# Attention with a feed-forward on one core: split reciprocals, a new order of products, an earlier first pair and earlier stores

## The chip, the core and the metric

The kernel runs on one core of a Trainium2 chip. TensorE multiplies matrices and writes its results to eight banks of PSUM; VectorE (DVE), ScalarE (ACT) and GpSimd (POOL) do the elementwise work, and GpSimd does not read PSUM here. SyncE (SP) and ACT issue DMAs. The metric is the device time of one execution in microseconds (us), less is better. All data are float32.

## The reference

```python
def rmsnorm(x, g):
    return x / np.sqrt(np.mean(x * x, axis=-1, keepdims=True) + 1e-06) * g
# q, k, v: (batch 8, heads 12, seq 448, dim 64)
scores = 1.0 / np.sqrt(64) * rmsnorm(q, g_q) @ rmsnorm(k, g_k).transpose(0, 1, 3, 2)
attn = np.exp(scores - scores.max(-1, keepdims=True))
attn = attn / (attn.sum(-1, keepdims=True) + 1e-09)
x = (attn @ v).transpose(0, 2, 1, 3).reshape(8 * 448, 768)
h = np.maximum(x @ w_in, 0.0)          # w_in (768, 2048)
out = h * h @ w_out                    # w_out (2048, 768)
```

## The kernel before, in words

**Two programs and a branch.** The kernel reads the gains `g_q` and `g_k`, multiplies them, and sets a flag when their largest product is small enough for exponentials without the subtraction of a maximum. Every engine loads the flag and branches (L67, L68). With this data the branch without `shift` runs.

**Attention.** 48 pairs of heads, i = 0 to 47, are worked on one after the other, each in two visits (n = 0 and 1) of two key chunks each. For a pair, SP loads q and k (`load_qk`, two pairs ahead), ACT squares them (`square`), VectorE sums the squares and GpSimd takes the power -1/2 and scales q (`normalize`); k's scale goes into the exponential instead. TensorE transposes q and k (`turn`, L178), VectorE and ACT copy the results out (`qT`, `kT`). `weigh` makes four scores matmuls per visit (L198) and ACT their exponentials (L200). One visit set later `attend` multiplies by the values (L244). Row sums of the weights come from matmuls with ones: for the first two batches chunk by chunk (L251), for the others (`alone` is false) from sums of the four chunks that `add_up` makes (L212), head 0 on GpSimd, head 1 on VectorE. `denominators` puts them into bank 3 (L259) and ACT copies that to `xT` (L263); `invert` takes the reciprocal on VectorE (L274) and `finish` multiplies the values by it, reading their bank (L283).

**Feed-forward.** Two batches are one group u, 0 to 3. Both matrix products use a scheme of seven products (Strassen's, in Winograd's form): `make_x_forms` makes the sums of the activations that it needs (L311, VectorE and GpSimd in turn), and the weights are converted from their loaded form once, during the first half of the run (`convert`: three ACT operations, four on VectorE, then sums and a store), and reloaded from DRAM in later groups. A group has four blocks. A block has two rounds of seven *first products* (`first_products`, three matmuls each, L382) whose results ACT copies (`part`, L389) or VectorE adds up to `hid` (`hidden`, L403, then Relu and Square on ACT, L404 and L405), and then *second products* (`second_products`: four parts for the rest rows, L428, sums of `hid`, L440, and three rounds of seven, two matmuls each, L452), which VectorE adds to `acc` (L485, L469; in block 0 ACT copies).

**Banks.** The products share banks 5 to 7 in three roles, listed first in `PRODUCTS`; a product with `first` false adds to what its bank holds. A bank may be written again once ACT or VectorE has read it. `turn_roles` says which bank has which role in the next round.

**The order.** It is written out by hand: each engine does its instructions in the program's order. Group u's products are a generator (`stream`), and the attention of the next two batches is spread among them: `run` draws products until a cost is reached, 18 for a first product and 10 for a second, and after each draws a conversion if one is due, x forms if a group of four `xT` is complete, and one task off the list `tasks`. `visit_among` does the matmuls and exponentials of a visit at once and puts VectorE's part on that list. A group costs 2008 and has 24 visits, so six lie in a block: two in its first products, one between first and second products, two in the second, one at its end. Pairs 0 to 11 run before any product (`visit_alone`), and group 3 runs alone at the end.

**Stores.** At the end of a group `store` writes the seven tiles `acc` (L496), all on SP.

Of the kernel before, what the change touches and what calls it, by code (L numbers as in the profile page):

```python
# [2 lines left out]

# [30 lines left out]
def kernel(  # L34
# [18 lines left out]
    D = q.shape[3]  # L53
    const = ctx.enter_context(tc.tile_pool(name="const", bufs=1))
    g_rows = const.tile([1, 2, D], F32, name="g_rows")
    g_most = const.tile([1, 1], F32, name="g_most")
    bounded = const.tile([1, 1], I32, name="bounded")
    for n, g in enumerate((g_q, g_k)):
        nc.scalar.dma_start(g_rows[:, n], g.rearrange("(one d) -> one d", one=1))
    nc.vector.tensor_tensor(out=g_rows[:, 0], in0=g_rows[:, 0], in1=g_rows[:, 1], op=ALU.mult)  # L60
    nc.vector.tensor_reduce(
        out=g_most, in_=g_rows[:, 0], axis=AX.X, op=ALU.max, apply_absolute_value=True
    )
    nc.vector.tensor_scalar(
        out=bounded, in0=g_most, scalar1=MOST_G, scalar2=None, op0=ALU.is_le
    )
    flag = nc.values_load(bounded, min_val=0, max_val=1)  # L67
    with tc.If(flag > 0) as either:  # L68
        program(tc, q, k, v, g_rows[:, 0], moe_w_in, moe_w_out, out, shift=False)
    with either.Else():  # L70
        program(tc, q, k, v, g_rows[:, 0], moe_w_in, moe_w_out, out, shift=True)
# [3 lines left out]
def program(ctx, tc, q, k, v, g_row, moe_w_in, moe_w_out, out, shift):  # L75
    nc = tc.nc

    B, H, S, D = q.shape
# [15 lines left out]
    small = ctx.enter_context(tc.tile_pool(name="small", bufs=8))  # L94
# [4 lines left out]
    ident = const.tile([P, P], F32, name="ident")  # L99
    ones = const.tile([CP, D], F32, name="ones")  # L100
    g = const.tile([P, 1], F32, name="g")
    minus_half = const.tile([CP, 1], F32, name="minus_half")
# [12 lines left out]
    loaded, values, squared, normal, turned = {}, {}, {}, {}, {}  # L115
# [7 lines left out]
    def load_qk(i):  # L123
        b, c = pairs[i]
        qk = io.tile([CP, 2, 2 * NJ, D], F32, name="qk", tag="qk")
        for x, rows in enumerate((q, k)):
            for e in range(2):
                nc.sync.dma_start(
                    qk[:, x].rearrange("p (j h) d -> p j h d", h=2)[:, :, e],
                    rows[b, 2 * c + e].rearrange("(p j) d -> p j d", j=NJ),  # L130
                )
        loaded[i] = qk
# [10 lines left out]
    def square(i):  # L143
        squares = [
            att.tile([CP, 2 * NJ, D], F32, name="squares", tag="squares") for _ in range(2)
        ]
        for x in range(2):
            nc.scalar.activation(squares[x], loaded[i][:, x], AF.Square)
        squared[i] = squares

    def normalize(i):

# [647 lines left out]
```

## Time and profile before

| what | before |
|---|---|
| median of 3 runs | 1597.87 us (1596.63 to 1598.27) |
| the profiled execution | 1598.84 us, span of its instructions 1597.0 us |
| granted TensorE clock, mean | 0.980 |
| reciprocals, L274 | 36 of 2946 ns, and 12 of 2953 ns (attention alone) |
| exponentials, L200 | 384 of 634 ns |
| bytes moved by DMA | 164.65 MB, 31.4% of 16 engines' span |

The page has one row for each engine's busy time. A row of waits reads: who waited, for what, us in total, how often, the longest. A row of a timeline reads: start, duration, engine, line, operation, tile written and tiles read, shapes, how many rows are merged, and in brackets how long the engine was idle before and what ended that. A matmul of the program is two rows in the trace, and its end is modelled, so a merged row ends a little after the next may start.

### The profile page before, as it was taken

Reading aid. Unit: us, or ns where it says so; the run is one execution under the profiler, and the core shown is the slowest. Engines: PE = TensorE matmul, PEld = TensorE weight load, DVE = VectorE, ACT = ScalarE, POOL = GpSimd, SP = SyncE. Lnnn points to the kernel's source line nnn. Section 1 sums busy time; section 2 is a strip of 40 time slices with the busy share of each in tenths; the row PEclk is TensorE's granted clock in tenths of the full one; section 3 lists DMA queues with packets and bytes.
Section 4 is the critical chain, followed back from the end, with each engine's and each line's share of the span. In section 5 each row is a group of like instructions: output and inputs, shape, how many; then the busy total and the mean of one; then the engine's idle time right before and its main releaser. Section 6 shows DMA issues by size and latency. Waiting matters only on the chain.

```text
span 1597.0 us, 14972 instructions
## 1 busy us (share of the span) xinstructions
PE 1508.5 (94%) x5204; PEld 733.1 (46%) x5204; DVE 845.9 (53%) x1234; ACT 632.9 (40%) x1197; POOL 450.1 (28%) x298
## 2 busy tenths in 40 slices
PE   5999999889889899999999989999999989999997
PEld 2333444344444344544445444544445444555554
DVE  3897685775876753535454554436446263223323
ACT  4775465725716224342342413433251412231130
POOL 3454542342332422323222332322232130000000
PEclk9999999999999999999999999999999999999999
DMA  4554143542533325132323206132230305132122
GB/s 101 168 150 160 43 120 94 176 135 67 186 122 126 106 76 168 44 131 64 101 89 106 95 12 206 55 105 93 96 104 6 120 34 183 41 142 84 65 79 72
DMA packets 131801, 164.65 MB, mean 103 GB/s; under 512 B 92804, under 2 KB 115844, under 8 KB 123524
## 3 DMA queue, kind: packets, MB, share of 16 engines
q1 hardware_dynamic: 131712, 163.60, 31.4%
q8 instruction: 43, 0.70, 0.2%
q14 instruction: 42, 0.34, 0.1%
q10 hardware_dynamic: 4, 0.00, 0.0%
HBM read 128.98 MB, written 34.60 MB: 102 GB/s over the span
## 4 chain that ended last, share of the span: by engine, by line
PE 81%; DVE 13%; ACT 2%; issue 2%; POOL 0%; SPq 0%; DMA 0%; ACTq 0%; DVEq 0%; POOLq 0%
PE bank L382 29%; PE bank L452 24%; PE bank L198 10%; PE bank L244 9%; PE bank L428 4%; DVE xT L274 3%; PE bank L251 2%; PE bank L178 2%; DVE acc L485 2%; PE bank L259 2%; DVE sum L212 1%; DVE xT L311 1%; DVE sums L440 1%; DVE hid L403 1%; DVE in_sb L567 1%
## 5 line engine op out<-in xcount | busy, mean ns | idle before, releaser
L382 PE MATMUL bank<-xT,in_sb 128*128 128x448 f32 x1344 | 526.7, 546 | 7.1 <-ACT part L389 7.1
L382 PEld LDWEIGHTS bank<-xT,in_sb 128*128 128x128 f32 x1344 | 251.6, 192 | 258.1 <-issue 244.8
L200 ACT ACTIVATE wT<-bank,rr 112x448 f32<-112x448 f32 x384 | 211.9, 634 | 339.5 <-PE bank L198 338.3
L485 DVE TENSOR_TENSOR acc<-acc,bank 128x384 f32<-128x384 f32 x324 | 173.2, 548 | 203.5 <-PE bank L452 170.1
L452 PE MATMUL bank<-out_sb,hid 128*128 128x384 f32 x768 | 268.2, 495 | 5.5 <-DVE acc L485 5.5
L452 PE MATMUL bank<-out_sb,sums 128*128 128x384 f32 x576 | 211.1, 510 | 30.7 <-DVE acc L485 29.4
L403 DVE TENSOR_TENSOR hid<-bank,part 128x448 f32<-128x448 f32 x96 | 59.9, 624 | 307.2 <-PE bank L382 178.6
L161 POOL TENSOR_TENSOR rr<-ms,minus_half 112x16 f32<-112x16 f32 x48 | 140.1, 2918 | 267.4 <-DVE ms L157 246.4
L452 PEld LDWEIGHTS bank<-out_sb,hid 128*128 128x128 f32 x768 | 144.8, 192 | 116.3 <-issue 18.9
L198 PE MATMUL bank<-qT,kT 64*112 64x448 f32 x768 | 179.5, 571 | 10.7 <-ACT xT L263 9.0
L244 PE MATMUL bank<-wT,vt 112*64 112x448 f32 x768 | 169.7, 552 | 3.3 <-DVE xT L283 3.3
L452 PEld LDWEIGHTS bank<-out_sb,sums 128*128 128x128 f32 x576 | 109.4, 197 | 115.5 <-DVE acc L485 40.8
L404 ACT ACTIVATE hid<-hid 128x448 f32<-128x448 f32 x128 | 73.8, 576 | 202.1 <-DVE hid L403 202.1
L212 POOL TENSOR_TENSOR sum<-wT 112x448 f32<-112x448 f32 x36 | 40.9, 1136 | 379.8 <-ACT wT L200 379.8
L389 ACT COPY part<-bank 128x448 f32<-128x448 f32 x128 | 67.9, 530 | 151.8 <-PE bank L382 151.8
L198 PEld LDWEIGHTS bank<-qT,kT 64*112 64x112 f32 x768 | 63.6, 175 | 114.8 <-issue 64.5
L212 POOL TENSOR_TENSOR sum<-sum,wT 112x448 f32<-112x448 f32 x72 | 83.0, 1153 | 110.1 <-ACT wT L200 107.2
L274 DVE RECIPROCAL xT<-xT 128x448 f32<-128x448 f32 x36 | 106.1, 2946 | 11.4 <-ACT xT L263 11.4
L440 POOL TENSOR_TENSOR sums<-hid,sums 128x768 f32<-128x768 f32 x16 | 29.9, 1866 | 240.8 <-DVE sums L440 240.8
L244 PEld LDWEIGHTS bank<-wT,vt 112*64 112x64 f32 x768 | 50.2, 137 | 97.1 <-issue 81.1
L428 PE MATMUL bank<-out_sb,hid 128*128 128x384 f32 x256 | 91.6, 514 | 0.0
L212 DVE TENSOR_TENSOR sum<-wT 112x448 f32<-112x448 f32 x36 | 37.5, 1041 | 96.3 <-ACT wT L200 96.3
(56 smaller groups left out, 1222.6 us busy)
## 6 DMA issues: line engine op xcount, KB each, us to landing
out_sb<-out_forms SPq DMA_DIRECT2D x24, 1536.0 KB, 7.3
in_sb<-in_forms SPq DMA_DIRECT2D x24, 1344.0 KB, 6.1
words<-in_moe_w_in_dram SPq DMA_DIRECT2D x32, 384.0 KB, 3.8
words<-in_moe_w_out_dram SPq DMA_DIRECT2D x32, 384.0 KB, 3.2
out_forms<-out_sb SPq DMA_DIRECT2D x8, 1536.0 KB, 6.9
qk<-in_q_dram SPq DMA_DIRECT2D x96, 112.0 KB, 3.0
qk<-in_k_dram SPq DMA_DIRECT2D x96, 112.0 KB, 3.1
vt<-in_v_dram SPq DMA_DIRECT2D x48, 224.0 KB, 3.9
```

The lines of the kernel that those rows point to most:

```text
L161: nc.gpsimd.tensor_tensor(out=rr.rearrange("p x r -> p (x r)"), in0=ms, in1=minus_half.to_broadcast([CP, 4 * NJ]), op=ALU.pow,)
L198: nc.tensor.matmul(sc, lhsT=kT[r, ts(m, CP)], rhs=qT[r, :], start=True, stop=True)
L200: nc.scalar.activation(weights[i, e, m], sc, AF.Exp, scale=normal[i][1][:, 2 * m + e : 2 * m + e + 1])
L212: engine.tensor_tensor(out=sums[i, e], in0=left, in1=weights[i, e, m], op=ALU.add)
L244: nc.tensor.matmul(av[ds(e * D, D), :], lhsT=values[i][:, e, m, :], rhs=weights[i, e, m], start=m == 0, stop=m == NJ - 1,)
L274: nc.vector.reciprocal(out=dens[i], in_=den)
L382: nc.tensor.matmul(ps, lhsT=w_sb[:, IN.index(left), c, :], rhs=forms[u, c][right], start=first and c == 0, stop=c == NK - 1, skip_group_ch ...
L403: nc.vector.tensor_tensor(out=dst, in0=left, in1=right, op=op)
L404: nc.scalar.activation(dst, dst, AF.Relu)
L428: nc.tensor.matmul(ps, lhsT=flat[a][:, t, ds(FULL, P)], rhs=w_sb[t][:, 2 * a + half, :], start=(a, t) == parts[0], stop=(a, t) == parts[-1],)
L452: nc.tensor.matmul(ps, lhsT=lefts[left][:, t, ts(tt, P)], rhs=w_sb[t][:, OUT.index(right), :], start=first and t == 0, stop=t == 1, skip_g ...
L485: nc.vector.tensor_tensor(out=acc, in0=acc, in1=ps, op=ALU.add)
```

## The change

1. **Ahead of the branch.** Identity, ones, the loads of pair 0 (q on SP, k on ACT's queue), a first Exp that loads ACT's table, and pair 0's norm are moved ahead of the flag. q and k of pair 0 get separate squares (in PSUM), means and powers of 8 numbers a row, and VectorE scales q. A class `Rows` holds loading and norm for both parts.
2. **Tasks.** A reciprocal is two, of 224 columns each, as two tasks; the norm is three tasks (mean of q, mean of k, power and scaling); all three additions of a head's weights are made after the second visit instead of one after the first and two after the second. After a first product two tasks are taken, after a second product one.
3. **Order of products.** In the first products P4 comes before P7; ACT copies P4 and both last sums follow P7. In the second P4 comes before P3. The roles turn so that two products lie between uses of a bank.
4. **Stores.** In a group's last block a tile is stored two or more products after its last addition. The very last tile goes out on SP and ACT.
5. **Pools.** `sum` has 2 buffers instead of 4, `ms` and `rr` 5 each, `squares` one for q and one for k.

```diff
+    rows = Rows(nc, SimpleNamespace(io=const, small=const), q, k, ones, minus_half)
+        rows.load(0, (nc.sync, nc.scalar))
+        nc.scalar.activation(g_most, ones[0:1, 0:1], AF.Exp)
+        make_identity(nc, ident)
...
+        for x in range(2):
+            rows.square(0, x, psum)
+            rows.add(0, x)
+            rows.power(0, ds(x, 1))
+            if x == 0:
+                rows.scale(0, x, nc.vector)
     flag = nc.values_load(bounded, min_val=0, max_val=1)
...
-        nc.vector.reciprocal(out=dens[i], in_=den)
+    def invert_half(i, half, den):
+        some = ds(half * (S // 2), S // 2)
+        nc.vector.reciprocal(out=dens[i][:, some], in_=den[:, some])
...
-    FIRST_ORDER = ["P1", "P5", "P2", "P6", "P3", "P7", "P4"]
+    FIRST_ORDER = ["P1", "P5", "P2", "P6", "P3", "P4", "P7"]
...
             elif name == "P7":
+                hidden(hid[1][:, 0], ps, copies["P4"], ALU.subtract)
                 hidden(hid[1][:, 1], ps, copies["P5"], ALU.add)
-            elif name == "P4":
-                hidden(hid[1][:, 0], copies["P7"], ps, ALU.subtract)
...
+                if name in ("P2", "P4") and blk == NBLK - 1:
+                    while to_store:
+                        store_rows(*to_store.popleft())
...
-            if tasks:
+            for _ in range(min(len(tasks), 2 if cost == COST_IN else 1)):
                 tasks.popleft()()
...
         if n and not shift:
-            tasks.append(lambda: invert(i - 1))
+            den = invert(i - 1)
+            tasks.append(lambda: invert_half(i - 1, 0, den))
+            tasks.append(lambda: invert_half(i - 1, 1, den))
             tasks.append(lambda: finish(i - 1))
-        if i <= last and not shift:
-            for m in range(2 * n or 1, 2 * n + 2):
+        if n and i <= last and not shift:
+            for m in range(1, NJ):
                 add_up(i, 0, m)
                 tasks.append(lambda m=m: add_up(i, 1, m))
...
-            tasks.append(lambda: normalize(i + 2))
+            tasks.append(lambda: rows.add(i + 2, 0))
+            tasks.append(lambda: rows.add(i + 2, 1))
+            tasks.append(lambda: rescale(i + 2))
```

TensorE, one round of first products near the end of group 3, before (P1, P5, P2, P6, P3, P7, P4; the number after `bank` tells the three banks apart):

```order
L382 MATMUL bank_7413<-xT,in_sb 128x448 x3
L382 MATMUL bank_7414<-xT,in_sb 128x448 x3
L382 MATMUL bank_7415<-xT,in_sb 128x448 x3
L382 MATMUL bank_7413<-xT,in_sb 128x448 x3
L382 MATMUL bank_7414<-xT,in_sb 128x448 x3
L382 MATMUL bank_7413<-xT,in_sb 128x448 x3
L382 MATMUL bank_7415<-xT,in_sb 128x448 x3
```

The same round now (P1, P5, P2, P6, P3, P4, P7; line 382 is line 449):

```order
L449 MATMUL bank_7516<-xT,in_sb 128x448 x3
L449 MATMUL bank_7515<-xT,in_sb 128x448 x3
L449 MATMUL bank_7517<-xT,in_sb 128x448 x3
L449 MATMUL bank_7516<-xT,in_sb 128x448 x3
L449 MATMUL bank_7515<-xT,in_sb 128x448 x3
L449 MATMUL bank_7517<-xT,in_sb 128x448 x3
L449 MATMUL bank_7516<-xT,in_sb 128x448 x3
```

The sixth and seventh have changed places: the bank that the fourth writes had one product between that and its next use, and now has two.

VectorE, at the last n = 1 visit of group 0, among second products, before (`acc` rows free a bank, the reciprocal and the two rows behind `finish`, L311 and L212, are tasks and x forms):

```order
L485 TENSOR_TENSOR acc<-acc,bank_127 128x384 x2
L274 RECIPROCAL xT<-xT 128x448
L485 TENSOR_TENSOR acc<-acc,bank_128 128x384
L283 TENSOR_TENSOR xT<-bank_125,xT 128x448
L485 TENSOR_TENSOR acc<-acc,bank_126 128x384
L311 TENSOR_TENSOR xT<-xT 128x448 x2
L212 TENSOR_TENSOR sum<-sum,wT 112x448
L485 TENSOR_TENSOR acc<-acc,bank_127 128x384
L212 TENSOR_TENSOR sum<-sum,wT 112x448
```

The same place now:

```order
L569 TENSOR_TENSOR acc<-acc,bank_160 128x384 x2
L345 RECIPROCAL xT<-xT 128x224
L569 TENSOR_TENSOR acc<-acc,bank_159 128x384
L345 RECIPROCAL xT<-xT 128x224
L569 TENSOR_TENSOR acc<-acc,bank_158 128x384
L354 TENSOR_TENSOR xT<-bank_157,xT 128x448
L569 TENSOR_TENSOR acc<-acc,bank_160 128x384
L382 TENSOR_TENSOR xT<-xT 128x448 x2
L279 TENSOR_TENSOR sum<-wT 112x448
L247 TENSOR_SCALAR qT<-bank_153,g 128x448
L569 TENSOR_TENSOR acc<-acc,bank_159 128x384
```

Between two additions to `acc` there is now half a reciprocal at most, and `finish`, the differences (L382 of the new code) and the additions of weights come one product later.

VectorE, where group 0 goes from the first to the second products of its last block, before:

```order
L311 TENSOR_TENSOR xT<-xT 128x448 x2
L212 TENSOR_TENSOR sum<-sum,wT 112x448
L485 TENSOR_TENSOR acc<-acc,bank_127 128x384
L212 TENSOR_TENSOR sum<-sum,wT 112x448
L485 TENSOR_TENSOR acc<-acc,bank_128 128x384
```

The same place now:

```order
L569 TENSOR_TENSOR acc<-acc,bank_160 128x384
L354 TENSOR_TENSOR xT<-bank_157,xT 128x448
L569 TENSOR_TENSOR acc<-acc,bank_159 128x384
L382 TENSOR_TENSOR xT<-xT 128x448 x2
L279 TENSOR_TENSOR sum<-wT 112x448
L569 TENSOR_TENSOR acc<-acc,bank_158 128x384
```

The second addition to `acc` of the parts now stands ahead of the two differences, not behind them and an addition of weights.

219 lines of the change are left out of this document (140 added, 79 removed).

## The prediction

> **What bounds the kernel now.** I read the page first, then TensorE's own waits, then the timelines around the longest of them.
>
> ```profile
> span 1597.0 us, 14972 instructions
> PE 1508.5 (94%) x5204; PEld 733.1 (46%) x5204; DVE 845.9 (53%) x1234; ACT 632.9 (40%) x1197; POOL 450.1 (28%) x298
> ...
> PE bank L452 <- DVE acc L485: 34.9, 20, 4.8
> PE bank L178 <- POOL qk L166: 17.4, 3, 11.7
> PE bank L198 <- ACT xT L263: 9.0, 6, 2.9
> PE bank L382 <- ACT part L389: 7.1, 3, 2.4
> PE bank L244 <- DVE xT L283: 3.3, 3, 1.1
> ```
>
> TensorE is busy for 94% of the span, and no edit takes a product from it. So the change can only win from the 88.5 us in which TensorE does nothing (1597.0 - 1508.5), and from what those pauses cost behind them. The five waits shown hold 71.7 us of it (each row: us in total, times, the longest). All but the second are waits for a PSUM bank that another engine has still to read. The rest is mostly the start and the end, where nothing can be multiplied.
>
> **The head.** The rows are in order of time: start, duration, engine.
>
> ```profile
> 3.03 0.14 DVE L64 TENSOR_SCALAR bounded<-g_most 1x1 int32<-1x1 f32 x1
> ...
> 3.83 1.41 SPq L128 DMA_DIRECT2D qk<-in_q_dram  x2
> ...
> 7.82 1.28 ACT L148 ACT_TABLE_LOAD   x1 [7.82 <-DMA qk<-in_q_dram]
> ...
> 9.78 0.69 DVE L156 TENSOR_REDUCE ms<-squares 112x8 f32<-112x512 f32 x1 [4.97 <-ACT squares L148]
> ...
> 12.18 2.91 POOL L161 TENSOR_TENSOR rr<-ms,minus_half 112x16 f32<-112x16 f32 x1 [7.73 <-DMA qk<-in_k_dram]
> ...
> 16.27 1.75 PE L178 MATMUL bank<-ident,qk 112*128 112x112 f32 x8 [11.67 <-POOL qk L166]
> ...
> 18.64 3.33 PE L198 MATMUL bank<-qT,kT 64*112 64x448 f32 x8 [0.62 <-ACT kT L182]
> ...
> 24.79 1.76 PE L178 MATMUL bank<-ident,qk 112*128 112x112 f32 x8 [2.82 <-POOL qk L166]
> ```
>
> Before, q is asked for at 3.83, behind the flag, and is there at 7.82, 4.0 us on. The table load (1.28) and the square lead to 9.78. In the changed kernel q's loads are SP's first instructions, at some 0.7 us, and k's go out on ACT's queue beside them; the table is loaded while they travel. So q is there at about 4.7, squared at 5.4 (9.78 - 7.82 - 1.28 = 0.68), and its mean is ready at 6.3. The power now takes 8 numbers a row instead of 16. No row shows that: its cost lies between 1.46 and 2.91. The work is done number by number, so I take 1.6. Scaling is now VectorE's: before, 1.2 us lie between the power's end (15.09) and the transposes (16.27); I take 0.7. That gives 8.6. But VectorE then has k's mean (0.9) and the branch (0.7, as from 3.17 to 3.83) before it may copy the transposed q (0.7): the first scores start near 11.2 instead of 18.64.
>
> What counts is the second pair, for which TensorE waits until 24.79. Its loads come later in the queue than one might think. The flag's line now waits for ACT, since the dummy Exp writes `g_most`, and ACT issues four loads and the table load first, so SP passes the branch near 5.7 instead of 3.83; one weight piece goes ahead of the pair. It lands near 12 all the same, and its squares stand behind the copy of k at 11. Mean, power (2.91) and scale bring its transposes to about 17.7. **I take 7.0 us**; 5.0 if the small power costs a full 2.91 and the loads crowd, 8.0 at best.
>
> **The end of the attention-only stage.**
>
> ```profile
> 154.64 1.14 DVE L212 TENSOR_TENSOR sum<-wT 112x448 f32<-112x448 f32 x1 [4.99 <-ACT wT L200]
> ...
> 161.93 0.60 PE L178 MATMUL bank<-ident,qk 112*128 112x112 f32 x4 [2.96 <-POOL qk L166]
> ```
>
> Here VectorE waits for an addition of weights that stands ahead of the norm of a later pair. The change moves that addition to the next visit, so the norm comes about 1.1 us sooner: **1.2**, between 0 and the whole 2.96. Two additions more then stand ahead of the x forms; the products that need them come 4 us later, which covers them.
>
> **Reciprocals among second products.**
>
> ```profile
> 763.10 2.95 DVE L274 RECIPROCAL xT<-xT 128x448 f32<-128x448 f32 x1
> ...
> 764.54 1.45 PE L452 MATMUL bank<-out_sb,sums 128*128 128x384 f32 x4
> ...
> 768.49 1.56 PE L452 MATMUL bank<-out_sb,sums 128*128 128x384 f32 x4 [0.43 <-DVE acc L485]
> ```
>
> A second product is four matmuls, 1.45 us with the pipeline's end in it, and VectorE must empty its bank (some 0.55). A reciprocal of 2.95 keeps it from that for two products. Between 764.54 and 768.49 lie 3.95 us, for two products and four transposes (0.6): a wait of 0.45, and near 1.0 if the three pipeline ends of some 0.2 overlap. With halves of 1.5 between the additions, VectorE falls behind by some 0.6 a product, twice, and the two products between uses of a bank (2.9) cover that. Six visits look like this. I take 0.8 for each, **5.0**; bounds 2.6 (the six visible 0.43) and 6.
>
> **First products of the first group.**
>
> ```profile
> 507.28 0.62 DVE L403 TENSOR_TENSOR hid<-bank,part 128x448 f32<-128x448 f32 x1 [4.64 <-ACT part L389]
> ...
> 510.14 2.95 DVE L274 RECIPROCAL xT<-xT 128x448 f32<-128x448 f32 x1
> ...
> 522.68 0.61 DVE L403 TENSOR_TENSOR hid<-bank,part 128x448 f32<-128x448 f32 x1
> ...
> 517.25 1.72 PE L244 MATMUL bank<-wT,vt 112*64 112x448 f32 x8 [1.11 <-DVE xT L283]
> ...
> 520.60 4.78 PE L382 MATMUL bank<-xT,in_sb 128*128 128x448 f32 x12
> ...
> 528.12 5.30 PE L382 MATMUL bank<-xT,in_sb 128*128 128x448 f32 x9 [2.36 <-ACT part L389]
> ...
> 527.52 0.54 ACT L389 COPY part<-bank 128x448 f32<-128x448 f32 x1
> ```
>
> VectorE idles 4.64 us until P7's copy is made, because P7's sum stands ahead of a weight conversion and the reciprocal. It then works without a gap until after 522.68, and everything behind is late: the value matmuls of line 244, whose bank `finish` reads, P2's sum, and through ACT's queue the copy of P6, on which P7 waits with one product between. In the new order P4 comes sixth and asks VectorE for nothing: conversion and reciprocal run in that gap. P7 is one product further from P6. So both waits go, three times each: 3.3 + 7.1 = 10.4. Behind the 2.36 us, nine matmuls take 5.30 where twelve took 4.78, which is 3.6 for nine: 1.7 us lost to a slower clock, three times 5.2. Together **15.6**. The 9.0 us for ACT's copy of the denominators (`xT` L263) I leave where they are: in two blocks VectorE and ACT have weights to convert without pause, and a TensorE that arrives sooner will wait longer there. Bounds: 4 and 21.
>
> [...]
>
> **The x forms.**
>
> ```profile
> 544.37 5.28 DVE L311 TENSOR_TENSOR xT<-xT 128x448 f32<-128x448 f32 x2
> 549.57 1.55 DVE L212 TENSOR_TENSOR sum<-sum,wT 112x448 f32<-112x448 f32 x1
> 551.04 0.54 DVE L485 TENSOR_TENSOR acc<-acc,bank 128x384 f32<-128x384 f32 x1
> ...
> 551.63 5.83 PE L452 MATMUL bank<-out_sb,sums 128*128 128x384 f32 x12 [4.65 <-DVE acc L485]
> ...
> 585.81 2.68 PE L452 MATMUL bank<-out_sb,sums 128*128 128x384 f32 x4 [2.56 <-DVE acc L485]
> ...
> 1328.03 1.56 PE L452 MATMUL bank<-out_sb,sums 128*128 128x384 f32 x4 [1.09 <-DVE acc L485]
> ```
>
> Three times (551.63 is one) two differences and an addition stand ahead of the addition that frees a bank, and TensorE stands 4.65 us. The differences still wait for GpSimd, but `finish` now comes a product later, so the bank's addition passes ahead of them. TensorE gets one product further and then waits for the next: I take 1.5 each, 4.5, between 0 and 3 each. At 585.81 reciprocal, differences and addition all fall within three products. Spread out, they leave about 1 us of the 2.56, and spare the half clock (2.68 for four matmuls against 1.45): some 3.6, twice, 7.2. In the last group 1.09 and what goes before it: 1.5. **13.2** in all, between 5 and 20.
>
> **What is lost.**
>
> ```profile
> 726.45 0.58 ACT L404 ACTIVATE hid<-hid 128x448 f32<-128x448 f32 x1 [0.73 <-DVE hid L403]
> ...
> 727.54 0.51 ACT L263 COPY xT<-bank 128x448 f32<-128x448 f32 x1
> ...
> 727.87 1.76 PE L198 MATMUL bank<-qT,kT 64*112 64x448 f32 x8
> ```
>
> Two sums now hang on P7, so at the middle of a block ACT has two activations more (1.16) before the copy of the denominators, which would end at 729.2. The last score matmuls need its bank; they start 0.9 after 727.87, so 0.3 late. Eight such places in the later groups: **-2.4**, between 0 and -9 (1.16 at each).
>
> **The tail.**
>
> ```profile
> 1587.48 1.02 DVE L485 TENSOR_TENSOR acc<-acc,bank 128x384 f32<-128x384 f32 x2 [0.73 <-PE bank L452]
> ...
> 1587.79 4.13 SPq L496 DMA_DIRECT2D out_dram<-acc  x6
> ...
> out_dram<-acc SPq DMA_DIRECT2D x8, 336.0 KB, 4.2
> ```
>
> The last sum is ready at 1588.50 (1587.48 + 1.02), but the last of six issues ends at 1591.92, and the span 5.1 us later. With only the last tile left, in two pieces on two queues, the last issue ends near 1589.1, 2.8 us sooner. With two tiles under way instead of five the landing (4.2 in the median for this size) should be quicker too: **3.5**, between 2.5 and 4.3.
>
> At nothing I cost: 48 more scalings of means on VectorE (0.17 each, in an engine that is 53% busy), smaller pools, stores among SP's loads (those are issued two tiles ahead), and weights held longer (their additions come well before the next pair's exponentials).
>
> **Sum.** 7.0 + 1.2 + 5.0 + 15.6 + 13.2 - 2.4 + 3.5 = 43.1. The profiled execution took 1598.84 us (span 1597.0 and 1.8 around it), 1.0 over the median of the runs: 1598.84 - 43.1 = 1555.7, and 1555 beside the runs' median of 1597.87.
>
> **Rivals.**
> First, *VectorE stays the bound of the first group*: products that come sooner only wait longer for its queue, and the x forms keep their waits.
>
> ```profile
> 286.00:303.00 17.00, 15.89 (x53) 7.27 (x52) 16.21 (x30) 10.27 (x21) 1.05 (x1) 1.00 0.46 164
> ```
>
> For it: in these 17 us of another block (busy time of TensorE, its weight loads, VectorE, ACT, GpSimd) VectorE works 16.21. Against it: the 4.64 us pause just before such a stretch. Then 15.6 shrinks to 3 and 13.2 to 5: 1555 + 20.8 = 1576.
>
> Second, *the head hardly shortens*, because the flag waits for the table and pair 1's loads land nearly as late as before: 2 instead of 7, 1555 + 5 = 1560.
>
> Third, on the other side: *GpSimd's three additions in a row hold VectorE*. The three, 3.4 us together, now all follow the second half of a pair's exponentials, just when halves and bank additions alternate. In the row at 544.37 two differences took 5.28, while the two additions at 549.57 took 1.55 and at 154.64 1.14. If every one of 36 visits lost more than 43.1 / 36 = 1.2 us so, the change would lose; at 2.0 each it gives 1555 + 72 = 1627. Against it: the same additions ran before, one visit sooner, and bank additions from PSUM kept 0.54 beside them. [...]
>
> Chances: forecast 0.64 (1540 to 1567), VectorE bound 0.22, head 0.09, GpSimd 0.05. The range takes in the first two rivals and the better bounds (8.0, 3.0, 6, 21, 20, 0 and 4.3 come to some 62, or 19 under the forecast): 1536 to 1577. A measurement tells about 0.2%, 3 us, from no change. Slower by more than that only in the third rival, 0.04; within, 0.02; faster 0.94.
>
> **What would show it.** Head: second pair's transposes near 18. Six waits of 0.43 gone; no wait of a first product for ACT's `part` over 1 us; waits for `acc` at the x forms under 4 us; the last store landing within 4.5 us of the last sum. Wrong I would be if TensorE's waits for ACT's copy `xT` grow above 15 us, or if VectorE's additions of weights on average double.

## The result and the profile after

The changed kernel takes **1561.36 us** (median, 1558.97 to 1562.85) against 1597.72 for the kernel before (1596.63 to 1598.27): a ratio of 0.9772, 95% interval 0.9755 to 0.9789. That is 36.4 us where 43.1 was forecast. Its profiled execution took 1561.56 us.

The head of the page of the changed kernel (span, then busy time of each engine):

```profile
span 1559.5 us, 15169 instructions
...
PE 1497.3 (96%) x5204; PEld 731.8 (47%) x5204; DVE 842.9 (54%) x1331; ACT 629.8 (40%) x1198; POOL 445.6 (29%) x298
```

TensorE's pauses shrank from 88.5 to 62.2 us (1559.5 - 1497.3). Its busy time fell too, by 11.2 us, with the same 5204 matmuls: fewer of them ran at half clock (mean granted clock 0.986, before 0.980). So of the 37.5 us of span, 26.3 are pauses and 11.2 are busy time. By the clock records of the two traces, 52.1 us of TensorE's busy time lay in stretches at half clock before and 36.2 do now, which makes some 8 of the 11.2; the rest is not explained here. TensorE's waits, as us in total, times, the longest:

```profile
PE bank L528 <- DVE acc L569: 26.5, 12, 4.1
PE bank L265 <- ACT xT L330: 10.0, 6, 4.1
PE bank L720 <- DVE ms L138: 9.8, 1, 9.8
PE bank L245 <- POOL qk L154: 5.2, 2, 3.1
PE bank L528 <- DVE sums L506: 2.3, 1, 2.3
PE bank L265 <- DVE qT L247: 1.2, 1, 1.2
```

In the changed file L528 is a second product, L449 a first one, L265 the scores, L245 the transposes, L569 an addition that empties a bank, L330 ScalarE's copy of the denominators, L279 an addition of weights, L382 a difference of the x forms. The waits of first products for `part` (7.1) and of L244 for `xT` (3.3) are gone, as forecast; twelve waits for `acc` are left of twenty; the wait for the copy `xT` went from 9.0 to 10.0. (The 9.8 us at the start took the place of longer ones, 11.7 for GpSimd and 4.2 for VectorE.)

**Where it came from.** I took the start of the same matmul in both traces and subtracted, product by product; the difference between two such landmarks is what a stretch gained. Grouped by the terms of the forecast:

| term | forecast | measured | how |
|---|---|---|---|
| head | 7.0 | 6.1 | first value product 29.74 to 23.67 |
| end of the attention-only stage | 1.2 | -0.9 | from there to the first product of the first group |
| reciprocals among second products | 5.0 | 8.3 | two visits in the first group 1.08 each, four later ones 1.53 |
| first products of the first group | 15.6 | 9.8 | blocks 1 to 3 gain 16.2, block 0 loses 6.4 |
| x forms | 13.2 | 14.6 | 1.25, 3.95, 0.83 and 3.21, 3.21, 2.11 |
| middle of the blocks, later groups | -2.4 | -3.2 | eight steps of 0.40 |
| tail | 3.5 | 3.0 | span's end minus last matmul's landmark |
| sum | 43.1 | 37.7 | the spans differ by 37.5 |

**The head**, in order of time (start, duration, engine):

```profile
3.11 1.28 ACT L73 ACT_TABLE_LOAD   x1 [3.11 <-issue]
4.88 0.14 DVE L79 TENSOR_SCALAR bounded<-g_most 1x1 int32<-1x1 f32 x1
...
6.64 1.65 POOL L147 TENSOR_TENSOR rr<-ms,minus_half 112x8 f32<-112x8 f32 x1 [5.34 <-DVE ms L141]
...
11.91 0.53 ACT L249 COPY kT<-bank 128x448 f32<-128x448 f32 x1 [5.73 <-PE bank L245]
12.34 1.15 ACT L133 ACTIVATE squares<-qk 112x512 f32<-112x512 f32 x2
...
18.91 1.75 PE L245 MATMUL bank<-ident,qk 112*128 112x112 f32 x8 [3.08 <-POOL qk L154]
```

The power of 8 numbers a row took 1.65 us (forecast 1.6; 16 had taken 2.91), and the second pair's transposes begin at 18.91 instead of 24.79 (forecast "about 17.7"). Its squares begin right behind the copy of k at 11.91, some 0.9 later than I had them.

**The one place that lost.** Two stretches of block 0 in the first group, from its first second product to the start of the second row tile; 49 matmuls each. The columns are busy times of TensorE, weight loads, VectorE, ScalarE, GpSimd, then the granted clock. Before, then after:

```profile
224.20:238.32 14.12, 13.04 (x49) 6.71 (x48) 13.17 (x19) 6.70 (x15) 5.48 (x3) 1.00 0.51 169
```

```profile
215.17:239.57 24.40, 17.99 (x49) 7.96 (x48) 16.60 (x24) 7.15 (x15) 6.26 (x4) 0.79 0.34 113
```

The same 49 matmuls take 10.3 us more. The timeline of the changed kernel there:

```profile
221.34 0.61 DVE L354 TENSOR_TENSOR xT<-bank,xT 128x448 f32<-128x448 f32 x1
...
221.88 1.91 DVE L279 TENSOR_TENSOR sum<-wT 112x448 f32<-112x448 f32 x1
...
224.10 1.84 DVE L651 TENSOR_SCALAR in_sb<-words 128x384 uint32<-128x384 uint32 x1
...
228.64 0.55 DVE L569 TENSOR_TENSOR acc<-acc,bank 128x384 f32<-128x384 f32 x1
...
229.24 2.93 PE L528 MATMUL bank<-out_sb,hid 128*128 128x384 f32 x4 [4.14 <-DVE acc L569]
```

The product at 229.24 is P4, now the fifth. It reuses the bank of P2, and P2's addition (228.64) is VectorE's, behind `finish`, an addition of weights and a weight conversion. Before, the fifth was P3, on the bank of P5, which in block 0 is copied by ScalarE. TensorE stands 4.14 us and then does four matmuls in 2.93 us, twice the usual 1.45.

**The tail** is as forecast: the last sum ends at 1553.92, both queues issue their last store at once, and the span ends 5.5 us after the sum (8.5 before).

```profile
1552.19 2.07 SPq L580 DMA_DIRECT2D out_dram<-acc  x3
1552.90 1.02 DVE L569 TENSOR_TENSOR acc<-acc,bank 128x384 f32<-128x384 f32 x2 [0.73 <-PE bank L528]
1553.95 0.39 ACTq L580 DMA_DIRECT2D out_dram<-acc  x1
```

### The profile page after: what moved, and what is told of

Same layout as the page of the kernel before. It is cut to its first block, busy times and chain, and to the rows that moved or that the text cites. A ratio compares the mean times of both kernels' runs of the same rounds, so it can differ in the third digit from the quotient of the medians.

```text
span 1559.5 us, 15169 instructions
## 1 busy us (share of the span) xinstructions
PE 1497.3 (96%) x5204; PEld 731.8 (47%) x5204; DVE 842.9 (54%) x1331; ACT 629.8 (40%) x1198; POOL 445.6 (29%) x298
## 4 chain that ended last, share of the span: by engine, by line
PE 85%; DVE 10%; ACT 2%; issue 2%; DMA 1%; POOL 0%; DVEq 0%; SPq 0%; ACTq 0%; POOLq 0%
PE bank L449 29%; PE bank L528 27%; PE bank L265 10%; PE bank L311 9%; PE bank L494 4%; PE bank L245 2%; PE bank L318 2%; PE bank L326 2%; DVE sum L279 1%; DVE xT L345 1%; DVE words L647 1%; DVE xT L382 1%; DVE acc L569 1%; DVE in_sb L651 1%; DVE out_sb L655 1%
## 5 line engine op out<-in xcount | busy, mean ns | idle before, releaser
L449 PE MATMUL bank<-xT,in_sb 128*128 128x448 f32 x1344 | 522.0, 543 | 0.0
L449 PEld LDWEIGHTS bank<-xT,in_sb 128*128 128x128 f32 x1344 | 250.1, 190 | 248.1 <-issue 234.7
L569 DVE TENSOR_TENSOR acc<-acc,bank 128x384 f32<-128x384 f32 x324 | 171.8, 545 | 223.6 <-PE bank L528 180.6
L528 PE MATMUL bank<-out_sb,hid 128*128 128x384 f32 x768 | 274.3, 495 | 17.5 <-DVE acc L569 17.5
L147 POOL TENSOR_TENSOR rr<-ms,minus_half 112x16 f32<-112x16 f32 (+1 forms) x49 | 139.8, 2854 | 500.0 <-DVE ms L141 499.8
L469 DVE TENSOR_TENSOR hid<-bank,part 128x448 f32<-128x448 f32 x128 | 76.6, 619 | 294.2 <-PE bank L449 274.6
L528 PE MATMUL bank<-out_sb,sums 128*128 128x384 f32 x576 | 210.6, 499 | 11.2 <-DVE acc L569 8.9
L528 PEld LDWEIGHTS bank<-out_sb,hid 128*128 128x128 f32 x768 | 145.0, 192 | 126.1 <-DVE acc L569 23.5
L265 PE MATMUL bank<-qT,kT 64*112 64x448 f32 x768 | 184.4, 575 | 11.9 <-ACT xT L330 10.0
L311 PE MATMUL bank<-wT,vt 112*64 112x448 f32 x768 | 170.1, 553 | 0.0
L470 ACT ACTIVATE hid<-hid 128x448 f32<-128x448 f32 x128 | 73.3, 572 | 206.5 <-DVE hid L469 206.5
L528 PEld LDWEIGHTS bank<-out_sb,sums 128*128 128x128 f32 x576 | 108.3, 193 | 89.8 <-issue 14.4
L345 DVE RECIPROCAL xT<-xT 128x224 f32<-128x224 f32 x72 | 108.1, 1528 | 29.7 <-ACT xT L330 29.7
L265 PEld LDWEIGHTS bank<-qT,kT 64*112 64x112 f32 x768 | 66.2, 176 | 118.0 <-issue 68.6
L138 DVE TENSOR_REDUCE ms<-squares 112x8 f32<-112x512 f32 x96 | 65.3, 680 | 92.8 <-ACT squares L133 92.8
L279 POOL TENSOR_TENSOR sum<-sum,wT 112x448 f32<-112x448 f32 x72 | 82.9, 1152 | 75.8 <-ACT wT L267 72.8
L311 PEld LDWEIGHTS bank<-wT,vt 112*64 112x64 f32 x768 | 50.2, 138 | 94.1 <-issue 80.8
L494 PE MATMUL bank<-out_sb,hid 128*128 128x384 f32 x256 | 89.5, 505 | 0.0
L471 ACT ACTIVATE hid<-hid 128x448 f32<-128x448 f32 x128 | 73.8, 577 | 4.0
```

The source lines that it names most:

```text
L147: self.nc.gpsimd.tensor_tensor(out=self.rr[i][:, which].rearrange("p x r -> p (x r)"), in0=ms, in1=self.minus_half.to_broadcast(list(ms.sh ...
L265: nc.tensor.matmul(sc, lhsT=kT[r, ts(m, CP)], rhs=qT[r, :], start=True, stop=True)
L279: engine.tensor_tensor(out=sums[i, e], in0=left, in1=weights[i, e, m], op=ALU.add)
L311: nc.tensor.matmul(av[ds(e * D, D), :], lhsT=values[i][:, e, m, :], rhs=weights[i, e, m], start=m == 0, stop=m == NJ - 1,)
L345: nc.vector.reciprocal(out=dens[i][:, some], in_=den[:, some])
L449: nc.tensor.matmul(ps, lhsT=w_sb[:, IN.index(left), c, :], rhs=forms[u, c][right], start=first and c == 0, stop=c == NK - 1, skip_group_ch ...
```

## The experiments

Each time is a median of five runs (four with whole reciprocals, eleven with the additions alone), compared with the changed kernel's 1561.36 where nothing else is said. They were measured in three sets at other times than the changed kernel; the kernel before, which ran beside each set, stayed at 1597.6 to 1598.1. Steps at landmarks are from one profiled execution each, and the slow stretches of the clock do not lie at the same place in each: a single step of 1 to 3 us counts only where the median or several places bear it out.

### The old order of second products

```diff
-    SECOND_ORDER = ["P1", "P2", "P5", "P6", "P4", "P3", "P7"]
+    SECOND_ORDER = ["P1", "P2", "P5", "P6", "P3", "P4", "P7"]
...
-            turn_roles(2, 0, 1)
+            turn_roles(1, 0, 2)
```

> The changed kernel with the second products in the old order (P3 fifth, P4 sixth, banks turned as before). Theory of the bank: in block 0 of group 0 the changed kernel loses 10.3 us between TensorE's landmarks, because P4, now fifth, waits 4.14 us for the bank of P2, which VectorE empties behind finish and conversions; before, the fifth was P3 on the bank of P5, which ScalarE copies in block 0. With the old order that wait goes with the half clock behind it, and block 0 loses 2 to 5 us instead of 10.3. At the x forms and among the reciprocals waits for acc come back, since again only one product lies between two uses of a bank: 5 to 12 us over the kernel. Total 1558 to 1566. Rival (VectorE's queue is simply longer there, whatever the order of the banks): block 0 still loses 9 us or more, and the total is 1566 or above.

Measured: 1569.73 us, 8.4 slower. Block 0's stretch is back to what it was:

```profile
216.25:232.54 16.29, 13.52 (x49) 6.54 (x48) 14.77 (x22) 6.67 (x15) 4.69 (x3) 1.00 0.43 147
```

16.3 us at full clock instead of 24.4 at 0.79; with 1.7 lost just ahead of it, the block is 6.4 us shorter. So the bank is the cause, not a longer queue alone. The rest was under-sized: behind block 0 this kernel loses 15.4 us, not 5 to 12, and so the total lies above the theory's 1566, in the rival's range, though the rival's mechanism is out. The waits for `acc` show it, with 25 where the changed kernel has 12:

```profile
PE bank L528 <- DVE acc L569: 30.8, 25, 4.0
```

Each of the four visits with a reciprocal in the later groups loses 1.07 to 1.09 of the 1.53 that it had won, although the reciprocals are still halves.

### Whole reciprocals

```diff
-            tasks.append(lambda: invert_half(i - 1, 0, den))
-            tasks.append(lambda: invert_half(i - 1, 1, den))
+            tasks.append(lambda: nc.vector.reciprocal(out=dens[i - 1], in_=den))
```

> The changed kernel with each reciprocal whole (about 2.95 us) as one piece of work instead of two halves. Theory of the halves: a whole reciprocal keeps VectorE from a bank for two products, so the six visits with a reciprocal among second products become 0.7 to 1.1 us longer each and the x forms of the second kind 1 to 3 us each: 1567 to 1575. Rival (two products between the uses of a bank cover a whole reciprocal as well): no visit moves by more than 0.3 us, total 1561 plus or minus 3.

Measured: 1577.22 us, 15.9 slower, a little over the theory's range. The four visits with a reciprocal in the later groups lose 0.88 each, within its 0.7 to 1.1; the places at the x forms lose up to 4 us (3.07 and 1.01 at the end of the second group's work). With the run before, this settles the reciprocals: of the 1.53 us a visit, **halves without the order keep 0.45, the order without halves keeps 0.65. Either alone brings less than half; only the two together clear the bank in time.**

### The old order of first products

```diff
-    FIRST_ORDER = ["P1", "P5", "P2", "P6", "P3", "P4", "P7"]
+    FIRST_ORDER = ["P1", "P5", "P2", "P6", "P3", "P7", "P4"]
...
-                hidden(hid[1][:, 0], ps, copies["P4"], ALU.subtract)
...
+            elif name == "P4":
+                hidden(hid[1][:, 0], copies["P7"], ps, ALU.subtract)
```

> The changed kernel with the first products in the old order (P7 sixth, P4 last, with its old sums and turn of banks). Theory of the order: three waits of about 2.4 us for ScalarE's part come back in group 0 with their slow matmuls (1.7 us each), and in part the waits for VectorE's xT; in return ScalarE's copy of the denominators comes about 1.2 us sooner, so the waits of 4.1 us for xT fall to about 2, and the six steps of 0.40 us lost in groups 1 and 2 go. Total 1564 to 1572. Rival (what the order saves in group 0 is given back at once at the waits for xT, because VectorE and ScalarE are the bound there): total 1561 plus or minus 2.

Measured: 1567.24 us, 5.9 slower. TensorE's waits of this kernel:

```profile
PE bank L449 <- ACT part L456: 7.3, 3, 2.4
PE bank L265 <- ACT xT L330: 5.4, 6, 2.4
...
PE bank L311 <- DVE xT L354: 3.3, 3, 1.1
```

The waits are as the theory had them: the three waits for `part` return (7.3 us, before the change 7.1), the three for `xT` too (3.3 in both), the waits for the copy of the denominators halve, and the steps of 0.40 in the later groups go. The slow matmuls that it expected behind each wait for `part` come at one of the three only, the second:

```profile
306.25 4.78 PE L449 MATMUL bank<-xT,in_sb 128*128 128x448 f32 x12 [2.42 <-ACT part L456]
...
413.64 6.39 PE L449 MATMUL bank<-xT,in_sb 128*128 128x448 f32 x12 [2.43 <-ACT part L456]
...
521.02 4.78 PE L449 MATMUL bank<-xT,in_sb 128*128 128x448 f32 x12 [2.42 <-ACT part L456]
```

The first group is 9.3 us longer, the rest wins 2.7 of it back.

### The additions alone, in the kernel before

```diff
-        if i <= last and not shift:
-            for m in range(2 * n or 1, 2 * n + 2):
+        if n and i <= last and not shift:
+            for m in range(1, NJ):
                 add_up(i, 0, m)
```

(and the same in the attention-only stage)

> The kernel before, with only the placing of the additions of weights changed: all three of a pair behind its second visit. Theory: nothing on the path moves but the end of the attention-only stage (about -1 us); 1594 to 1599. Rival (three GpSimd additions in a row hold VectorE's instructions, and the changed kernel pays for that): 1603 or more, with longer VectorE sums and differences in the row of lines.

Measured: 1601.87 us, ratio 1.003 to the kernel before (1.002 to 1.004): between the two. It costs some 4 us in the median, with runs from 1597.7 to 1606.1; in the profiled execution, whose span is 3.0 us longer, block 0 of the first group loses 3.2. But not by the rival's mechanism. The group of VectorE's second and third additions (busy time in all, mean ns of one) in the kernel before and in this one:

```profile
L212 DVE TENSOR_TENSOR sum<-sum,wT 112x448 f32<-112x448 f32 x72 | 70.8, 983 | 0.8
```

```profile
L212 DVE TENSOR_TENSOR sum<-sum,wT 112x448 f32<-112x448 f32 x72 | 63.2, 878 | 1.1
```

They got shorter (and in the changed kernel shorter still, 696), which fits GpSimd's three being done by then. What it loses is place in VectorE's queue, three additions in a visit that had two. That is read from the trace, not tried by itself.

### The old order in block 0 only

```diff
-            for name in SECOND_ORDER:
+            early_block = u == 0 and blk == 0
+            for name in OLD_ORDER if early_block else SECOND_ORDER:
...
-            turn_roles(2, 0, 1)
+            turn_roles(*((1, 0, 2) if early_block else (2, 0, 1)))
```

> The changed kernel, with the old order of second products in block 0 of group 0 alone. The run with the old order everywhere was 7.0 us ahead of the changed kernel behind block 0 and lost 15.4 us after it. If the two parts are independent, this one keeps the 7.0 and none of the loss: 1553 to 1557. Rival (VectorE's queue, not the bank, holds block 0, and what is won there is lost at the next waits for VectorE and ScalarE in block 1): 1559 to 1562.

Measured: 1553.32 us, 8.0 faster than the changed kernel. The gain stays; it isn't lost at the next wait. In the profiled execution, whose span is 9.8 us shorter, block 0 gains 6.4, just what it had lost, and most of the rest (2.7) lies at the x form near the end of the third group, where the clock differs (see the last section). The mended place is the one that the forecast had missed.

### The x forms' differences in two pieces

```diff
+        differences.append(lambda: subtract((nc.vector, t1, b12, b11), (nc.gpsimd, t3, b22, b12)))
+        differences.append(lambda: subtract((nc.vector, t2, b22, t1), (nc.gpsimd, t4, t2, b21)))
```

(one of the two is taken after each product)

> The changed kernel with the four differences of the x forms in two pieces, one product apart, instead of all at once. Theory: at the x forms TensorE waits for acc (22.4 us of the 26.5 in all, the rest being block 0) because VectorE's second difference stands stretched beside GpSimd's, ahead of the addition that frees the bank; with a bank addition between the two, each wait loses 1 to 2 us: 1549 to 1556. Rival (the second difference is as long when it comes later, so the wait only moves by one product): 1560 to 1564.

Measured: 1554.11 us, 7.3 faster. One x form near the end of the third group, in the changed kernel and then here:

```profile
1260.57 4.16 DVE L382 TENSOR_TENSOR xT<-xT 128x448 f32<-128x448 f32 x2
...
1264.64 1.55 DVE L279 TENSOR_TENSOR sum<-wT 112x448 f32<-112x448 f32 x1
1266.12 0.54 DVE L569 TENSOR_TENSOR acc<-acc,bank 128x384 f32<-128x384 f32 x1
...
1266.71 2.93 PE L528 MATMUL bank<-out_sb,sums 128*128 128x384 f32 x4 [3.13 <-DVE acc L569]
```

```profile
1261.06 0.54 DVE L570 TENSOR_TENSOR acc<-acc,bank 128x384 f32<-128x384 f32 x1
1261.52 1.08 DVE L380 TENSOR_TENSOR xT<-xT 128x448 f32<-128x448 f32 x1
...
1261.65 1.56 PE L529 MATMUL bank<-out_sb,sums 128*128 128x384 f32 x4 [1.67 <-DVE acc L570]
```

Two differences in one piece hold VectorE 4.16 us, and with the addition behind them the bank is reached 5.55 us after they began. Apart, the bank's addition goes between, TensorE waits 1.67 instead of 3.13, and it stays at full clock behind (four matmuls 1.56 instead of 2.93). Of the 3.5 us that this place gains, 1.5 are the shorter wait; the rest is mostly clock, and the last section shows that the clock there can differ with no change of the wait. The expectation put 22.4 us of waits down to the x forms, which is too much: in the changed kernel's trace four waits of 9.7 us together, from 329 to 441 us, lie where no x form is made.

### The denominators half a visit sooner

```diff
+                if n and i and not shift and not alone(i - 1):
+                    denominators(i - 1)
                 run(COST * x / unit)
```

> The changed kernel with the denominators' two matmuls and ScalarE's copy half a visit sooner, ahead of the block's last first products. Theory: the six waits of 10.0 us for ScalarE's xT at the middle of a block (4.16 and 4.14 the longest) are ScalarE's queue, where two more activations and the conversion of weights stand ahead of that copy; copied half a visit sooner it never is late: those waits fall under 2 us together, the slow clock behind the two long ones goes (1.7 us each), and the eight steps of 0.40 us in groups 0 to 2 come back: 1546 to 1552. Rival (VectorE is the bound in group 0, and TensorE then waits as long for its sums or banks): only the steps of 0.40 come back, 1556 to 1560.

Measured: 1564.77 us, 3.4 slower: both expectations missed. The six waits for `xT` are gone altogether, and the second and third block of the first group reach their second products 7 to 10 us ahead of the changed kernel, only to lose most of that at once:

```profile
PE bank L528 <- DVE acc L569: 37.1, 11, 9.7
```

The stretch around one of the two longest of these waits (columns as above):

```profile
315.00:342.00 27.00, 16.61 (x53) 8.32 (x52) 23.32 (x35) 8.68 (x17) 8.84 (x7) 0.81 0.40 137
```

VectorE works 23.3 of 27 us there, conversions, both halves and the sums of `hid` ahead of the bank's addition. So in the middle of these two blocks my first rival's mechanism does hold: **VectorE is the bound, and the wait for ScalarE's copy was only the first to show it.** It does not explain the loss, though. At the end of the first group this kernel is still 3.9 us ahead of the changed one (1.0 of them it had when the group began). It falls behind in the later groups, where there was little to win: the two matmuls, now alone among products, cost 0.33 us at some twenty places, and one x form at the end of the second group loses 1.8.

### GpSimd's additions one by one

```diff
-                add_up(i, 0, m)
-                tasks.append(lambda m=m: add_up(i, 1, m))
+                tasks.append(lambda m=m: (add_up(i, 0, m), add_up(i, 1, m)))
```

> The changed kernel with GpSimd's three additions of a pair issued one by one with VectorE's, instead of all three in a row behind the visit. The additions alone, moved in the kernel before, had cost 3.0 us of span, nearly all in block 0 of group 0. If the three in a row are what stretches VectorE there (1.84 us for a shift of words that takes 0.36 elsewhere), block 0 gets 2 to 4 us shorter: 1556 to 1560. Rival (what counts is how many additions fall into the stretch, not how they are spaced): 1560 to 1563.

Measured: 1558.72 us, 2.6 faster, in the first theory's range but not for its reason: block 0 moves by 0.6 only, the first group as a whole is 4.3 longer, and the gain lies at the x forms of the second and third (1.8 and 4.5). The three in a row are not what holds block 0.

### The flag

```diff
-        nc.scalar.activation(g_most, ones[0:1, 0:1], AF.Exp)
+        nc.scalar.activation(warm, ones[0:1, 0:1], AF.Exp)
```

> The changed kernel with the dummy Exp writing a tile of its own, so that the flag's line no longer waits for ScalarE's table load. In the changed kernel the flag is ready at 4.88 us, before the change at 3.03. Theory: the branch, the weight piece and the second pair's loads behind it come 1 to 1.8 us sooner, and the second pair's transposes, for which TensorE waits, by 0.5 to 1.5: 1559.5 to 1561. Rival (the second pair hangs on ScalarE's queue or on the loads under way, not on the branch): no step moves by more than 0.3 us, 1561 plus or minus 1.

Measured: 1561.09 us, no difference. The second pair's loads are issued 1.2 us sooner (5.33 instead of 6.51), but its transposes start only 0.32 sooner (18.59 instead of 18.91), as much as ScalarE's copy of k does (11.60 instead of 11.91). So the second pair hangs on ScalarE, not on the branch; the dummy Exp that holds up the flag costs nothing.

### The stores behind the last product

```diff
-                if name in ("P2", "P4") and blk == NBLK - 1:
-                    while to_store:
-                        store_rows(*to_store.popleft())
...
+        for e in range(2):
+            for t in range(NT):
+                store(accs[2 * t + e], [(2 * u + e, REST * e + P * t, P)], (nc.sync, nc.sync))
```

> The changed kernel with the stores of a group behind its last product, all on SP's queue, as before the change. Theory: only the end moves. From VectorE's last sum to the end of the span lay 8.55 us before and 5.54 in the changed kernel, so 3.0 us longer: 1563.5 to 1565.5. Rival (stores that come earlier also free accumulators or move other transfers, so something else in the kernel moves too): a step of over 0.5 us at the first products of a group.

Measured: 1564.39 us, 3.0 slower, and no landmark at the first products of a later group moves. In the profiled execution the span ends 9.77 us after the last sum, 4.2 later than in the changed kernel (5.54), and TensorE is 1.0 ahead from the first group on; the runs lie between 1562.2 and 1566.4, so the size is good to some 1 us. The stores' new place is worth the tail and nothing else.

### Three edits together, and a fourth

Block 0's order, the split differences and the flag in one kernel; then GpSimd's additions one by one on top.

> The changed kernel with three edits together: the old order of second products in block 0 of group 0, the x forms' differences in two pieces, and the dummy Exp in a tile of its own. Alone the first two had given 8.0 and 7.3 us against the changed kernel's median of 1561.4. If they act at different places and add up: 1543 to 1549. Rival (both take time from the same waits for VectorE in group 0): 1550 to 1553.

> As the run of three edits, with GpSimd's additions one by one as well, which alone had given 2.6 us, mostly at x forms of later groups. If those are the same waits that the split differences shorten, it adds nothing: within 1.5 us of the run of three edits. If the spacing acts by itself: 2 to 3 us less than it.

Measured: **1545.65 us** with three, 0.9671 of the kernel before (0.9658 to 0.9684), 15.7 faster than the changed kernel: the 8.0 and 7.3 add up. It beats both kernels. With the fourth it is 1559.53, 13.9 slower, though that edit alone had won 2.6; neither expectation held. The same x form at the end of the first group with three edits, then with four:

```profile
527.89 1.08 DVE L381 TENSOR_TENSOR xT<-xT 128x448 f32<-128x448 f32 x1
...
528.90 0.61 DVE L280 TENSOR_TENSOR sum<-sum,wT 112x448 f32<-112x448 f32 x1
...
530.62 1.56 PE L532 MATMUL bank<-out_sb,hid 128*128 128x384 f32 x4 [1.04 <-DVE acc L573]
```

```profile
532.87 1.51 POOL L280 TENSOR_TENSOR sum<-wT 112x448 f32<-112x448 f32 x1
533.32 2.63 DVE L280 TENSOR_TENSOR sum<-sum,wT 112x448 f32<-112x448 f32 x1
534.35 1.12 POOL L381 TENSOR_TENSOR xT<-xT 128x448 f32<-128x448 f32 x1
...
536.47 0.54 DVE L573 TENSOR_TENSOR acc<-acc,bank 128x384 f32<-128x384 f32 x1
...
537.06 2.93 PE L532 MATMUL bank<-out_sb,hid 128*128 128x384 f32 x4 [3.06 <-DVE acc L573]
```

Spaced out, GpSimd's addition runs beside VectorE's, which takes 2.63 us instead of 0.61 and ends only behind GpSimd's next instruction; the bank's addition comes late, TensorE waits 3.06 and goes on at half clock. Over the kernel VectorE's second and third additions take 878 ns on average instead of 699, its first ones 930 instead of 1026. So at this place VectorE is held beside GpSimd, and with three edits, where GpSimd's additions are issued in a row, it is not. This x form makes 1.5 of the 12.0 us by which the span is longer; the other places, most of them in the first group too, were not looked at one by one. Why the spacing won 2.6 us where the differences were in one piece stays open.

## Why the prediction was right, and where it was off

The time lies in the range (1536 to 1577), on the forecast's side, 6.4 us over the value. By its steps:

- **Head, 7.0.** Right: 6.1. The small power, VectorE's scaling and the two queues did what was said. TensorE starts later than forecast, though: its first matmul waits until 9.76 for VectorE's mean of k, so q's transposes begin at 10.07, not 8.6. The second pair, which counts, is 1.2 late. The second rival, a head that hardly shortens because of the flag, is out by this and by the run on the flag.
- **End of the attention-only stage, 1.2.** Wrong in sign, -0.9. The norm does come sooner (TensorE's wait 2.96 to 2.08), but the moved addition, which "the products that need them come 4 us later" was to cover, stands ahead of `qT` too (1.12 us, with the two that stood there before), and the scores wait 1.19 us for it. On VectorE it is one addition more, not "two": the other is GpSimd's. I had looked at the x forms behind, not at the copy between.
- **Reciprocals, 5.0.** Right in mechanism, under-sized: 8.3, over the bound of 6 (and six times 0.8 is 4.8, not 5.0). That came from the one visible wait and my count of pipeline ends in a visit, and the visits in the later groups hold a second such place. Both parts are needed, as two runs show.
- **First products of the first group, 15.6.** This is the term that was off: 9.8. For blocks 1 to 3 it holds (16.2, with luck in the clock, see the last section), and the old order brings the forecast's waits back as they were. Block 0 loses 6.4. The forecast valued the new order of *second* products only by how many products lie between uses of a bank; it did not ask which engine empties the bank. In block 0 ScalarE does it for P5 and VectorE for P2, and the new order exchanged the two. The run with the old order there alone is 8.0 us faster, and in its trace block 0 gains the 6.4 back.
- **x forms, 13.2.** Right, 14.6. One reading was off: at 585.81 the terms that are named, 1.56 of the wait and 1.23 of the clock, come to 2.8, not 3.6; measured were 3.21 each. What was left of these waits (3.13 us at the longest) was under the 4 named. Splitting the differences took another 7.3 us, so their price was more than the addition behind them.
- **Loss at the middle of blocks, -2.4.** Right: eight steps of 0.40 for 0.3, so 3.2 (729.2 less the 728.77 at which the scores would start is 0.4 as well). "A TensorE that arrives sooner will wait longer there" held too, 10.0 for 9.0, under the 15 that would have spoken against me.
- **Tail, 3.5.** Right, 3.0. The edit on its own costs 3.0 when undone. SP's part of the last tile lands 2.7 us after the last sum, within the 4.5 that were named; the landing of ACT's part is not in the trace, and the span ends 5.5 after the sum.
- **Costed at nothing:** the stores among loads move no landmark; the smaller pools were not tried by themselves. The additions' new place was not free: some 4 us in the kernel before.
- **First rival, VectorE the bound.** Half true: not where the order of first products acts, but at the middle of two blocks of the first group, as the run with early denominators shows. **Third rival:** its sign for VectorE's additions was the other way (983 to 696 ns).

## What to carry to other kernels

When an order of products is changed, list for each bank not only how many products lie between its uses but which engine empties it in each block, and what stands in that engine's queue. Two edits that relieve one queue (a shorter piece of work, one more product of slack) may each bring less than half of what they bring together, so undo each alone before crediting either. A wait that vanishes in the trace is worth its time only if no other engine is full behind it: read the busy time of each in that stretch first.

## What was not expected of the hardware

**Half clock after short waits, in stretches of 3.4 and 6.8 us.** The wait ahead of the first, and three stretches of the changed kernel (length, TensorE's busy time, granted clock, share and rate of DMA):

```profile
220.58 4.51 PE L528 MATMUL bank<-out_sb,sums 128*128 128x384 f32 x8 [2.27 <-DVE sums L506]
...
221.40:224.80 3.40, 3.40 (x7) 0.50 0.79 335
224.80:228.20 3.40, 0.29 (x1) 1.00 0.01 2
228.20:235.00 6.80, 5.76 (x12) 0.50 0.32 92
```

The stretch from 221.4 follows a wait of 2.27 us, shorter than the stretch itself; the one from 228.2 begins inside the next wait, of 4.14. In the trace's clock records they are 3413 and 6827 ns long. From the start of one half-clock stretch of this trace to that of the next lie whole multiples of 3413 ns (19 from 156.55 to 221.40, 2 more to 228.23, 26 to 316.97).

Nor does a wait of some length always cost the clock. At the x form near the end of the third group TensorE waits 3.13 us in the changed kernel and then needs 2.93 for four matmuls (shown with the split differences). In the run with the old order in block 0 it waits as long there, and goes on at full clock:

```profile
1259.61 1.56 PE L530 MATMUL bank<-out_sb,sums 128*128 128x384 f32 x4 [3.15 <-DVE acc L571]
```

What makes the difference was not shown. The waits for `part` agree: in the kernel before they were 2.37, 2.39 and 2.36 us long, and all three were followed by half clock (5.89 us for eleven matmuls, 6.47 and 6.43 for twelve, against 4.78); with the old order of first products they were 2.42, 2.43 and 2.42, and only the second was (6.39). So the 1.7 us that the forecast added behind each of these waits is not a fixed price; that it could be counted three times is partly luck.

**A one-input instruction held beside GpSimd.** The timeline of the changed kernel once more:

```profile
223.27 2.46 POOL L506 TENSOR_TENSOR hid<-hid 128x768 f32<-128x768 f32 x1
...
230.02 0.36 DVE L651 TENSOR_SCALAR in_sb<-words 128x384 uint32<-128x384 uint32 x1
```

The shift of words that takes 0.36 us at 230.02 took 1.84 at 224.10 (shown above), beside GpSimd's 2.46, and at 230.02 GpSimd had stood idle since 225.7; bank additions with an input in PSUM stayed at 0.54 to 0.55 in all of these stretches. So here it was not only VectorE's additions and differences of two tiles that took longer beside GpSimd.
